# The pools of a Mamba-2 and SiLU kernel in another order in SBUF

## The chip, the cores and the metric

One core of one Trainium2 chip runs the whole program. The metric is device time in microseconds of one execution; a kernel's time is the median of its runs. Profiles are of one execution, taken by the hardware profiler; all engines' times below are from the profile of the kernel before.

## What is computed

First a state-space scan over chunks of the sequence (4 batches, 8 heads, 768 steps, head size 32, state size 16), then two matrix products with a SiLU between them:

```python
for c in range(nc):                       # chunks; log_a = log(clip(a))
    cum = np.cumsum(la, axis=-1)
    L = np.exp(cum[:, :, :, None] - cum[:, :, None, :]) * causal
    M = np.einsum('bhin,bhjn->bhij', Cc, Bc) * L
    y_intra = np.einsum('bhij,bhjd->bhid', M, xc)
    y_inter = np.einsum('bhin,bhnd->bhid', Cc, state) * np.exp(cum)[..., None]
    y[:, :, sl] = y_intra + y_inter
    ...
    state = decay_full[:, :, None, None] * state + np.sum(Bx, axis=2)
x = y.transpose(0, 2, 1, 3).reshape(3072, 256)
h = x @ w_in                              # 256 x 2048
out = (h * (1.0 / (1.0 + np.exp(-h)))) @ w_out    # 2048 x 256
```

x, a, B and C come as float32; the weights come as eight-byte floats, which the kernel turns into float32 on the chip.

## The kernel before

The 3072 tokens are 12 units u of 256 tokens, and 6 pairs G of two units. A unit goes through the scan (f_E, f_B, f_T, f_T2, f_C, f_G, f_M, f_S, f_Y, with small plain-fp32 matmuls at L449, L463, L515 and L524) and ends as a tile ys of outputs. The sixteen weight pieces are loaded into tiles raw (load_w, L210), turned to float32 on ScalarE, VectorE and GpSimd (w_size, w_bits, w_add), and split into parts h, l and d (w_high, w_part), each part of 128x512 numbers in an s2k tile.

The first pair is computed in plain fp32: f_s1 (L573) and f_n2 (L604). All other pairs use fp32r parts. f_XH and f_XL split ys into three xk tiles. s1_mm (L645) multiplies them with the parts of w_in into the PSUM tiles ga and gb: per matmul, 128x128 weights from an s2k slot are held and 512 columns of an xk tile move. ScalarE makes the SiLU and a first part of it (f_a L653, f_d L660, f_h L666), VectorE the two other parts (L531, L534), all in r4k tiles. s2_mm (L626) multiplies these with the parts of w_out into hp and o_ps: again 128x128 weights from an s2k slot, 512 moving columns, now of an r4k tile. There are 480 matmuls at L645 and 480 at L626. f_va, f_vd and f_out (L632, L638, L586) add, transpose and store the result.

The order of everything is written out by hand in the string SCHEDULE: every token is one step, and the steps of all engines and DMA queues are issued in that order. The program is told not to reorder it.

A tile lies in a pool. A pool is a stretch of SBUF; a name (or tag) in it has a number of slots (bufs) that its tiles use in turn. Pools lie one behind the other in the order in which they are opened, and the names of a pool in the order of their first tile, each slot padded to 32 bytes. What goes into which pool, in bytes per partition:

| pool | tiles |
|---|---|
| const | tiny 4, ident 512, diag 2048, hm 32, par 8, one 1040 |
| loads | tbc 2048, bn 1024, pz 1040 |
| loads2 (2 slots each) | ab 4096, xt 2048 |
| rawp (7 slots) | raw 4096; xk uses the same slots |
| sc | ct 1024, ce 2048, cw 1024, BT 1024, bh 1024, sm 1024, bxs 1024, pfx 1040, ys 2048 |
| sc2 (2 slots) | st 1024 |
| sp (49 slots) | s2k, 2048 |
| rp (12 slots) | r4k, 4096 |

In the compiled program of before the first pool starts at byte 16512 of a partition. All slots of s2k and r4k start at 832 modulo 2048; raw (and so xk), ab, xt and ct at 1824; tbc and bn at 1792; ys and st at 832 and up.

Of the kernel before, what the change touches and what calls it, by code (L numbers as in the profile page):

```python
# [8 lines left out]
FP32 = mybir.dt.float32  # L9
# [62 lines left out]
def kernel(  # L72
# [24 lines left out]
    batch, H, S, D = x.shape  # L97
    N = B.shape[-1]
    Q = 64
# [7 lines left out]
    assert (H * N, H * D, D, N) == (128, 256, 32, 16) and S % UT == 0 and d_model == H * D  # L107

    const = ctx.enter_context(tc.tile_pool(name="const", bufs=1))
    loads = ctx.enter_context(tc.tile_pool(name="loads", bufs=1))  # L110
    loads2 = ctx.enter_context(tc.tile_pool(name="loads2", bufs=2))
    rawp = ctx.enter_context(tc.tile_pool(name="rawp", bufs=7))
    sc = ctx.enter_context(tc.tile_pool(name="sc", bufs=1))
    sc2 = ctx.enter_context(tc.tile_pool(name="sc2", bufs=2))
    sp = ctx.enter_context(tc.tile_pool(name="sp", bufs=49))
    rp = ctx.enter_context(tc.tile_pool(name="rp", bufs=12))
    dram = ctx.enter_context(tc.tile_pool(name="dram", bufs=1, space=bass.MemoryType.DRAM))
    ps_s = ctx.enter_context(tc.tile_pool(name="ps_s", bufs=1, space=bass.MemoryType.PSUM))
    ps_h = ctx.enter_context(tc.tile_pool(name="ps_h", bufs=3, space=bass.MemoryType.PSUM))
# [10 lines left out]
    def small(shape, dtype=FP32):  # L130
        return sp.tile(shape, dtype, name="s2k", tag="s2k")
# [7 lines left out]
    bn, tbc, xt, E, M, BT, BH, CT, CE, CW, PFX, ST, SM, DP, BX, YS, PZ = ({} for _ in range(17))  # L139
# [122 lines left out]
    pz01, one01, pfx01 = (large([128, 8 * (Q + 1)]) for _ in range(3))  # L262
    idle = small([128, 512], BF16)
    diag1 = small([128, 1, Q])
    tiny = const.tile([128, 1], FP32, name="tiny")
    ident = const.tile([128, 128], FP32, name="ident")
    diag = const.tile([128, H, Q], FP32, name="diag")
    hm = const.tile([128, H], FP32, name="hm")
    par = const.tile([128, 2], FP32, name="par")
    one = const.tile([128, 4, Q + 1], FP32, name="one")  # L270

    def i_a(l):
        nc.sync.dma_start(out=ach[:, l], in_=bass.AP(tensor=a.tensor, offset=a.offset + l * S,
# [88 lines left out]
            PFX[u] = pfx01.rearrange("p (c t) -> p c t", c=8)[:, 4 * u:4 * u + 4]  # L362

    def f_P(u):
        PFX[u] = sc.tile([128, 4, Q + 1], FP32, name="pfx")
        nc.vector.tensor_tensor_scan(out=PFX[u].rearrange("p c t -> p (c t)"),
                                     data0=PZ[u].rearrange("p c t -> p (c t)"),
                                     data1=one.rearrange("p c t -> p (c t)"), initial=0.0,
                                     op0=ALU.mult, op1=ALU.add)
# [304 lines left out]
    def f_e(G, i):  # L674
# [17 lines left out]
        "ia": i_a, "ip": i_p, "ir": i_r, "ci": c_idle, "ct": c_tiny, "cI": c_ident, "c1": c_diag1, "cd": c_diag,  # L692
        "cp": c_p01, "ch": c_hm, "cP": c_par, "co": c_one, "ca": c_acp, "A": f_A, "AT": f_AT, "AA": f_AA,
        "z": busy, "as": f_AS, "ab": f_Ab, "E": lambda u, *k: f_E(u, k or (0, 1)), "P01": f_P01, "P": f_P,
        "T": f_T, "tp": f_TP, "ce": f_T2, "B": f_B, "C": f_C, "D": lambda u: f_D0(u, True), "g0": f_G0, "G": f_G,
        "b": f_BX, "M": f_M, "S": f_S, "SM": f_SM, "Y": f_Y, "X0": f_X0, "y": f_YS, "xh": f_XH, "x": f_XL,
# [42 lines left out]
```

## Time and profile before

| what | value |
|---|---|
| runs | 345.09, 345.49, 347.36 us; median 345.49 |
| profiled execution, first to last instruction (span) | 345.5 us |
| mean granted TensorE clock | 0.995 |
| VectorE busy | 227.3 us |
| ScalarE busy | 218.5 us |
| moved by DMA | 35.03 MB in 99625 packets |
| first matmul of f_s1 (L573) | at 27.0 us |
| last matmul starts | at 338.5 us |

The span of the profiled execution equals the median of the runs to the tenth, so nothing that has to be counted lies around it. "out<-in xN" names the tile that is written, the tiles that are read, and the number of instructions; PEld is the loading of weights, which runs beside the matmuls. In the groups, the first number behind the bar is busy time in us, the second the mean duration of one in ns; then follows the idle time of the engine ahead of them. In the timeline, the first column is the start in us and the second the time until the last of the row ends; neighbouring matmuls overlap.

### The profile page before, as it was taken

The numbers are of one execution on the slowest core, as the hardware profiler recorded it, in microseconds if no ns is written. First come the engines' busy times: TensorE is split into PE (matmuls) and PEld (weight loads), VectorE is DVE, ScalarE is ACT, GpSimd is POOL, SyncE is SP. The second block draws the span as 40 slices with busy tenths as digits, with TensorE's granted clock in tenths as the row PEclk, the third lists the DMA queues.
The fourth block names the chain that finished last, engine by engine and source line by source line (L and its number), as shares of the span: only waits on it lengthen the run. The fifth ranks groups of instructions, "written<-read, shape, count | busy, mean of one in ns | idle before, by whom it ended". The sixth has DMA issues, their size and how long they took to land.

```text
span 345.5 us, 7609 instructions
## 1 busy us (share of the span) xinstructions
PE 330.6 (96%) x3081; PEld 248.8 (72%) x3082; DVE 227.3 (66%) x310; ACT 218.5 (63%) x339; POOL 75.8 (22%) x96
## 2 busy tenths in 40 slices
PE   5789999999999999999999999999999999999992
PEld 2467875566578777777787787778787788887881
DVE  3957679776356777389778577677675844554553
ACT  3576776757789786775755844647746645557330
POOL 1555336868341245201100010000001000000000
PEclk9999999999999999999999999999999999999998
DMA  5999799799993795985052550561000030012003
GB/s 135 206 198 293 190 300 185 135 166 182 202 157 61 153 177 95 147 154 108 14 91 76 80 107 3 92 138 18 2 0 2 3 60 2 0 29 33 0 0 61
DMA packets 99625, 35.03 MB, mean 101 GB/s; under 512 B 82488, under 2 KB 88632, under 8 KB 99592
## 3 DMA queue, kind: packets, MB, share of 16 engines
q1 hardware_dynamic: 91640, 25.71, 36.7%
q0 software_dynamic: 4784, 8.59, 14.4%
q10 hardware_dynamic: 3168, 0.26, 0.6%
q8 instruction: 24, 0.39, 0.5%
q14 instruction: 9, 0.07, 0.1%
HBM read 22.81 MB, written 3.34 MB: 76 GB/s over the span
## 4 chain that ended last, share of the span: by engine, by line
PE 85%; SPq 5%; DVE 3%; DMA 2%; issue 2%; POOL 1%; ACT 0%; DVEq 0%; POOLq 0%
PE hp L626 27%; PE ga L645 16%; PE gb L645 16%; PE hp L604 8%; PE o_ps L626 5%; PE hp L573 5%; SPq L210 1%; PE ga L463 1%; SPq L176 1%; PE ga L515 1%; PE ga L524 1%; POOL s2k L236 1%; DMA raw<-in_moe_w_in_dram 1%; PE ga L449 1%; PE gb L524 1%
## 5 line engine op out<-in xcount | busy, mean ns | idle before, releaser
L626 PE MATMUL hp<-r4k,s2k 128*128 128x512 f32 x400 | 115.2, 396 | 0.0
L626 PEld LDWEIGHTS hp<-r4k,s2k 128*128 128x128 f32 x400 | 74.3, 188 | 18.3 <-issue 1.3
L531 DVE SCALAR_TENSOR_TENSOR r4k<-r4k 128x1024 fp32r<-128x1024 f32 x40 | 48.8, 1231 | 31.6 <-ACT r4k L666 25.1
L645 PE MATMUL ga<-xk,s2k 128*128 128x512 f32 x240 | 63.9, 401 | 0.5 <-DVE st L494 0.2
L534 DVE SCALAR_TENSOR_TENSOR r4k<-r4k 128x1024 fp32r<-128x1024 f32 x40 | 48.5, 1222 | 22.3 <-ACT r4k L666 20.9
L645 PE MATMUL gb<-xk,s2k 128*128 128x512 f32 x240 | 62.5, 396 | 0.0
L645 PEld LDWEIGHTS ga<-xk,s2k 128*128 128x128 f32 x240 | 44.6, 188 | 13.3 <-ACT bxs L475 2.0
L645 PEld LDWEIGHTS gb<-xk,s2k 128*128 128x128 f32 x240 | 44.7, 188 | 11.3 <-ACT gb L653 0.4
L666 ACT ACTIVATE r4k<-r4k 128x1024 fp32r<-128x1024 f32 x40 | 41.6, 1054 | 0.5
L653 ACT ACTIVATE ga<-ga 128x1024 f32<-128x1024 f32 x20 | 20.2, 1008 | 29.5 <-PE ga L645 29.4
L247 POOL DMA_DIRECT2D s2k<-s2k x32 | 28.7, 1008 | 44.5 <-ACT s2k L245 33.5
L573 PE MATMUL hp<-r4k,s2k 128*128 128x256 f32 x128 | 31.9, 403 | 0.5 <-POOL s2k L236 0.5
L653 ACT ACTIVATE gb<-gb 128x1024 f32<-128x1024 f32 x20 | 20.2, 1008 | 18.4 <-PE gb L645 18.1
L626 PE MATMUL o_ps<-r4k,s2k 128*128 128x512 f32 x80 | 31.0, 394 | 0.0
L573 PEld LDWEIGHTS hp<-r4k,s2k 128*128 128x128 f32 x128 | 25.5, 203 | 7.2 <-issue 2.2
L604 PE MATMUL hp<-r4k,s2k 128*128 128x512 f32 x64 | 29.8, 599 | 0.0
L660 ACT ACTIVATE r4k<-ga 128x1024 f32<-128x1024 f32 x20 | 20.5, 1025 | 13.0 <-PE ga L645 12.3
L396 DVE TENSOR_TENSOR_SCAN ab<-ab,diag 128x512 f32<-128x512 f32 x20 | 25.8, 1309 | 3.2 <-DMA ab<-az 3.2
L236 POOL TENSOR_TENSOR s2k<-s2k 128x512 uint32<-128x512 uint32 (+1 forms) x19 | 24.4, 1318 | 15.6 <-DVE s2k L227 15.6
L404 POOL TENSOR_TENSOR BT<-bn,ab 128x256 f32<-128x256 f32 x10 | 8.3, 833 | 86.5 <-PE ga L645 33.7
L660 ACT ACTIVATE r4k<-gb 128x1024 f32<-128x1024 f32 x20 | 20.5, 1026 | 9.7 <-PE gb L645 8.4
L481 DVE TENSOR_TENSOR ab<-ga,ab 128x512 f32<-128x512 f32 x12 | 8.3, 690 | 18.3 <-PE gb L463 14.2
(111 smaller groups left out, 387.9 us busy)
## 6 DMA issues: line engine op xcount, KB each, us to landing
s2k<-s2k POOLq DMA_DIRECT2D x32, 256.0 KB, 4.7
ab<-az SPq DMA_DIRECT2D x20, 256.0 KB, 5.9
raw<-in_moe_w_in_dram SPq DMA_DIRECT2D x8, 512.0 KB
raw<-in_moe_w_out_dram SPq DMA_DIRECT2D x8, 512.0 KB, 5.3
out_dram<-r4k SPq DMA_DIRECT2D x44, 64.0 KB, 2.0
xt<-in_x_dram SPq DMA_DIRECT2D x20, 128.0 KB, 4.2
pz<-ac SPq DMA_DIRECT2D x10, 130.0 KB
bn<-in_B_dram SPq DMA_DIRECT2D x20, 64.0 KB
```

What stands on the lines that cost most here:

```text
L236: nc.gpsimd.tensor_tensor(out=dst[:, :, fs].bitcast(U32), in0=u[:, :, fs], in1=v[:, :, fs], op=ALU.add)
L247: nc.gpsimd.dma_start(out=f32(t).rearrange("p k f -> p (k f)"), in_=other.rearrange("p k f -> p (k f)"), accum_op=ALU.add)
L396: nc.vector.tensor_tensor_scan(out=o, data0=src, data1=diag.rearrange("p h t -> p (h t)"), initial=0.0, op0=ALU.mult, op1=ALU.add)
L531: nc.vector.scalar_tensor_tensor(out=l, in0=f32(h), scalar=BACK, in1=y, op0=ALU.mult, op1=ALU.add)
L534: nc.vector.scalar_tensor_tensor(out=d, in0=f32(h), scalar=-(BACK + 1.0), in1=y, op0=ALU.mult, op1=ALU.subtract)
L573: nc.tensor.matmul(out=hp[:, i], lhsT=WT[j][:, kc, 128 * i:128 * i + 128], rhs=XM[:, 2 * kc:2 * kc + 2, u], start=(kc == 0), stop=(kc == K ...
L604: nc.tensor.matmul(out=NP["o"][m], lhsT=WT[8 + f // 2][:, f % 2, 128 * m:128 * m + 128], rhs=GT[0, f // 2][:, f % 2], start=(f == 0), stop ...
L626: nc.tensor.matmul(out=ACC[P, 2 * (p == "d") + m], lhsT=WK[8 + f // 2, p][:, f % 2, 128 * m:128 * m + 128], rhs=rhs, start=(f == 0 and p ! ...
L645: nc.tensor.matmul(out=o, lhsT=WK[j, q][:, kc, 128 * i:128 * i + 128], rhs=xs[:, 2 * kc:2 * kc + 2], start=(start and q == "h" and kc == 0 ...
L653: nc.scalar.activation(t, t, AF.Copy, scale=1.0 + Z)
L660: nc.scalar.activation(g, t, AF.Silu, scale=BACK)
L666: nc.scalar.activation(t, GT[G, i], AF.Copy, scale=-LESS * Z)
```

## The change

The pools are opened in another order, and the tiles of const are made ahead of the other pools. A tile of 256 bytes that nobody uses fills const up; diag gets a pool of its own behind rp; pfx moves from sc to loads. Each instruction, each DMA and each wait stays, in the same order. Only the addresses in SBUF are others.

```diff
     const = ctx.enter_context(tc.tile_pool(name="const", bufs=1))
-    loads = ctx.enter_context(tc.tile_pool(name="loads", bufs=1))
-    loads2 = ctx.enter_context(tc.tile_pool(name="loads2", bufs=2))
+    tiny = const.tile([128, 1], FP32, name="tiny")
+    ident = const.tile([128, 128], FP32, name="ident")
+    hm = const.tile([128, H], FP32, name="hm")
+    par = const.tile([128, 2], FP32, name="par")
+    one = const.tile([128, 4, Q + 1], FP32, name="one")
+    const.tile([128, 64], FP32, name="pad")
     rawp = ctx.enter_context(tc.tile_pool(name="rawp", bufs=7))
-    sc = ctx.enter_context(tc.tile_pool(name="sc", bufs=1))
-    sc2 = ctx.enter_context(tc.tile_pool(name="sc2", bufs=2))
     sp = ctx.enter_context(tc.tile_pool(name="sp", bufs=49))
     rp = ctx.enter_context(tc.tile_pool(name="rp", bufs=12))
+    const2 = ctx.enter_context(tc.tile_pool(name="const2", bufs=1))
+    diag = const2.tile([128, H, Q], FP32, name="diag")
+    loads2 = ctx.enter_context(tc.tile_pool(name="loads2", bufs=2))
+    sc2 = ctx.enter_context(tc.tile_pool(name="sc2", bufs=2))
+    sc = ctx.enter_context(tc.tile_pool(name="sc", bufs=1))
+    loads = ctx.enter_context(tc.tile_pool(name="loads", bufs=1))
...
     def f_P(u):
-        PFX[u] = sc.tile([128, 4, Q + 1], FP32, name="pfx")
+        PFX[u] = loads.tile([128, 4, Q + 1], FP32, name="pfx")
```

More of the change, by code (lines that the diff above doesn't have):

```diff
@@ L264 @@
     diag1 = small([128, 1, Q])
[L265 to L270, printed above, removed]
     def i_a(l):
```

## The prediction

> **What bounds the kernel now.** I read the page first, then the windows by stage, then the timeline of TensorE, then the chain at the start. The page says that the kernel is one long TensorE stream at nearly full clock:
>
> ```profile
> span 345.5 us, 7609 instructions
> PE 330.6 (96%) x3081; PEld 248.8 (72%) x3082; DVE 227.3 (66%) x310; ACT 218.5 (63%) x339; POOL 75.8 (22%) x96
> PE 85%; SPq 5%; DVE 3%; DMA 2%; issue 2%; POOL 1%; ACT 0%; DVEq 0%; POOLq 0%
> L626 PE MATMUL hp<-r4k,s2k 128*128 128x512 f32 x400 | 115.2, 396 | 0.0
> L645 PE MATMUL ga<-xk,s2k 128*128 128x512 f32 x240 | 63.9, 401 | 0.5 <-DVE st L494 0.2
> L645 PE MATMUL gb<-xk,s2k 128*128 128x512 f32 x240 | 62.5, 396 | 0.0
> L626 PE MATMUL o_ps<-r4k,s2k 128*128 128x512 f32 x80 | 31.0, 394 | 0.0
> ```
>
> PE is on 85% of the chain, and the idle column of its large groups is near zero. The mean of 396 ns is one matmul from entry to end; matmuls overlap, so what counts is the distance from one start to the next. The timeline gives it. Two stretches, the first of L645 and then L626, the second of L626 alone:
>
> ```profile
> 198.21 2.03 PE L645 MATMUL gb<-xk,s2k 128*128 128x512 f32 x8
> 200.08 2.03 PE L645 MATMUL ga<-xk,s2k 128*128 128x512 f32 x8
> 201.94 1.09 PE L626 MATMUL hp<-r4k,s2k 128*128 128x512 f32 x4
> 202.87 0.39 PE L626 MATMUL o_ps<-r4k,s2k 128*128 128x512 f32 x1
> ```
> ```profile
> 217.35 0.39 PE L626 MATMUL hp<-r4k,s2k 128*128 128x512 f32 x1
> 217.58 0.39 PE L626 MATMUL o_ps<-r4k,s2k 128*128 128x512 f32 x1
> 217.81 1.30 PE L626 MATMUL hp<-r4k,s2k 128*128 128x512 f32 x5
> 218.94 0.39 PE L626 MATMUL o_ps<-r4k,s2k 128*128 128x512 f32 x1
> 219.17 1.07 PE L626 MATMUL hp<-r4k,s2k 128*128 128x512 f32 x4
> ```
>
> The reader is to divide. Sixteen L645 take 201.94 - 198.21 = 3.73 us, 233 ns each. Eight L626 take 219.17 - 217.35 = 1.82 us, 227.5 ns each. The four L626 straight after L645 take 0.93 us, 232 ns each. Both are the same instruction: 128 rows, 512 contiguous fp32r columns, 128x128 weights from s2k, full clock. Taken over the whole trace, by the starts of neighbours (steps under 260 ns, so no waits): 468 steps after an L645 have mean 233.2 ns and alternate between 235 and 232; 445 steps after an L626 have mean 229.6; and L626 from the sixth place of a run on has mean 227.3. The first five places after an L645 run have medians 230, 235, 228, 232 and 230. Neither the half of the tile, nor the quarter of the weights, nor the bank, nor what DVE, ACT or POOL do at that moment explains more than a nanosecond of it. What does differ is where the moving operand lies. In the compiled program of before, s2k and r4k start at 832 modulo 2048 (0 modulo 64); raw, from whose slots xk comes, starts at 1824 modulo 2048 (32 modulo 64).
>
> The start, up to the first L573 at 27 us, hangs on SyncE's issues and on DMAs. This is the sum by line of the chain from 0 to 27 us:
>
> ```profile
> by line: SPq L210 19.0%; SPq L176 18.5%; DMA raw<-in_moe_w_in_dram 16.3%; DMA s2k<-in_x_dram 11.0%; SPq L281 8.7%; SPq L191 7.9%; SPq L273 5.8%; issue 4.2%; DVE st L496 3.2%; PE hp L449 2.5%; DVEq L496 0.2%
> ```
>
> **The change part by part.** Nothing is removed or added: each instruction, DMA, wait and queue position stays; no step moves past another on any queue. Only addresses differ. Pools start at byte 16512. The new const holds 32 + 512 + 32 + 32 + 1056 + 256 = 1920 bytes, so rawp starts at 18432 = 9 x 2048, sp at 47104 = 23 x 2048, rp at 147456 = 72 x 2048; diag, ab, xt, st follow on multiples too, then sc, then loads. One thing falls short of the words: in sc the order of first use is ct (1024 bytes), then ce (2048), so ce lands 1024 past a multiple. It is read by short L463 matmuls and I cost that at nothing.
>
> 1. L645, moving operand from 1824 to 0 modulo 2048. 480 matmuls. After the change their operands stand to each other as L626's do now (moving start and weight slot equal modulo 2048), and both start on a multiple of 64. I take L626's settled step: 480 x (233.2 - 227.3) = 2.8 us less. Bounds: no gain (if the address is not the cause), or an estimate from the plain fp32 matmuls: L573 and L604 take 0.84 ns per column (216 for 256, 430 for 512), L626 0.444; half of 0.84 is 0.42, or 215 ns for 512, which I take as the lower end: 480 x 18.2 = 8.7 us. I take 227.3, the nearest row, same form and same engine state.
>
> 2. L626, from 832 to 0 modulo 2048. Its 229.6 is 227.3 plus the slow first places after L645. If L645 no longer leaves the stream in another rhythm, these go: 480 x 2.3 = 1.1 us less. Bounds: 0 (the first places after a pause are slow as well, 231, 235, 229, 232, so part of it may be a refill that any change of line brings), and 480 x (229.6 - 215) = 7.0 us by the same lower end. I take 1.1, since the pattern follows L645 on 55 occasions and pauses on 14.
>
> 3. Plain fp32 matmuls, L573 and L604: 216 and 430 ns, 0 modulo 64 already. Nothing. Small ones (L449, L463, L515, L524) sit 6 to 7 ns apart and together take some 24 us after 42 us; their operands come from 32 to 0 modulo 64. Their steps are set by issue, four at a time; the bounds are nothing and, at the 2.5% of point 1, 0.6 us. I take nothing.
>
> 4. DVE, ACT and POOL work on the same tiles. The like copies L245 (s2k to s2k, 624 ns) and L557 (ys to xk, 629 ns) differ by 5 ns, and L557 is the one at 32 modulo 64: nothing per instruction, at most 10 x 5 ns. DVE is busy 66% and ACT 63% beside a PE that does not wait for them: in the windows from 280 to 320 us PE is never idle. If PE runs 1.2% faster, what is late next is the chain ACT L653, L660, L666, DVE L531, L534; it has over 30% of slack in these windows and the order of the program keeps several items ahead, so I charge nothing. Without that cover, every late item costs what the 340 ns steps do now, some 100 ns each, 14 of them in L626.
>
> 5. DMA into raw, s2k, r4k, xt, bn. After 42 us hidden behind PE. Before 27 us it is on the path: the first raw load 4.41 us, and SyncE issues of up to 2.38 us that stand behind a busy queue. Bounds: none, or a tenth of the roughly 15 us that wait for DMA, 1.5 us either way, taken from the spread of equal raw loads (4.8 to 5.8 us to landing). I take nothing. [...]
>
> Sum against the profiled span of 345.5, which equals the median of the runs shown (345.49): 345.5 - 2.8 - 1.1 = 341.6, less a little that 3 and 5 may add. I say 341.5.
>
> **Rivals.**
>
> *The address is not the cause, 345.3.* L645 differs from L626 in more than the address: it goes on in one two-bank tile, and its weights step by 1024 bytes. For it: I have no row with the same line at two addresses. Against it: same-bank and other-bank neighbours of L626 differ by 0.4 ns, of L645 by 0.7. [...]
>
> *Alignment beyond 64 pays too, 330.* L626 now starts 64 past a multiple of 128 and 256. Should its own 227.3 fall to 215 as well: 8.7 + 7.0 = 15.7 us, 330. For it: 12 ns per matmul that twice the rate of plain fp32 would not have. Against it: nothing says that fp32r must reach exactly that rate, and no row starts on 128 or more.
>
> *Equal residues collide, slower.* All 68 large slots now begin at one residue, raw among them, so the moving stream, the weight load and DVE and ACT on other slots more often stand at the same place. If each 128x512 lost one more step of 5.9 ns: 960 x 5.9 = 5.7 us, 351. It decides from a mean step above 231.4 ns (the present mean of both lines); 1% slower is 235.0. Against it: s2k and r4k share 832 now, and that is the fast line; steps of L626 do not grow when DVE or ACT is busy (fitted 0.2 and 0.6 ns).
>
> **How the numbers follow.** Forecast (340.3 to 342.4 for itself) 0.50; no effect 0.22; deeper alignment 0.14; collision 0.14. The predicted time is the first. A measurement here tells about 1% from no change, so 342.0 and 349.0 are the lines. The forecast gives faster in three of four (0.38), the rest within 1%; deeper gives 0.14 faster. Together faster 0.52, within 1% 0.34, slower 0.14. The range goes from 337.0, a little beyond half of a deeper gain (345.5 - 7.9 = 337.6), to 347.0, which holds no effect with a DMA loss of 1.5 us; it leaves out most of deeper and of collision, 0.2 in all.
>
> **What would show it.** Right: L645's start-to-start step at 227 to 228 and no slow places behind it, L626 at 227 to 228, starts of the first L573 within 1 us of 27, no new wait of PE. Wrong: L645 still at 233 (rival one), L626 under 225 (two), any of them above 235 (three); a new row of PE waiting for ACT L653 or DVE L534 would say that the cover of point 4 was thinner than I took it, and a first L573 moved by over 1 us that point 5 was.

## The result, and the profile after

The changed kernel takes 341.46 us (median of 4, 340.02 to 343.88), the kernel before 345.29 (median of 4, 344.78 to 347.36): ratio 0.9871, 95% interval 0.9832 to 0.9910. Run once more with more rounds (341.50 against 346.36) the ratio is 0.9867, interval 0.9844 to 0.9889. So it is faster by 1.3%, some 4 us. The ratios below leave out one execution of 372.9 us, of the third kernel of the experiments, in which TensorE was granted 0.83 of its clock.

One reading of the time before has to be mended. A run's time is 2.0 us more than its span: 340.9 and 338.9 us for the profiled execution after, 346.5 and 344.5 for a second profile of the kernel before. The execution before that was profiled with a span of 345.5 therefore took about 347.5 us, two above the median. The two first profiles differ by 6.6 us of span; the medians differ by only about four.

These are the lines of the page after that answer to those of before. Line numbers have moved by two: L626 is L628, L645 is L647, L573 is L575.

```profile
span 338.9 us, 7609 instructions
PE 322.5 (95%) x3081; PEld 245.0 (72%) x3082; DVE 227.0 (67%) x310; ACT 218.2 (64%) x339; POOL 75.8 (22%) x96
PE 86%; SPq 5%; DVE 3%; issue 2%; POOL 1%; DMA 1%; ACT 0%; DVEq 0%; POOLq 0%
L628 PE MATMUL hp<-r4k,s2k 128*128 128x512 f32 x400 | 114.5, 395 | 0.0
L647 PE MATMUL ga<-xk,s2k 128*128 128x512 f32 x240 | 62.7, 396 | 0.5 <-DVE st L496 0.2
L647 PE MATMUL gb<-xk,s2k 128*128 128x512 f32 x240 | 61.2, 390 | 0.0
L628 PE MATMUL o_ps<-r4k,s2k 128*128 128x512 f32 x80 | 30.9, 393 | 0.0
```

TensorE lost 8 us of busy time, 3.3 of them in the four fp32r groups shown, the rest in the first pair and the start. DVE, ACT and POOL kept theirs to 0.3 us. The two stretches of the timeline that answer to those of before:

```profile
193.81 1.98 PE L647 MATMUL gb<-xk,s2k 128*128 128x512 f32 x8
195.63 1.98 PE L647 MATMUL ga<-xk,s2k 128*128 128x512 f32 x8
197.44 1.07 PE L628 MATMUL hp<-r4k,s2k 128*128 128x512 f32 x4
198.35 0.39 PE L628 MATMUL o_ps<-r4k,s2k 128*128 128x512 f32 x1
198.57 1.30 PE L628 MATMUL hp<-r4k,s2k 128*128 128x512 f32 x5
199.71 0.61 PE L647 MATMUL ga<-xk,s2k 128*128 128x512 f32 x2
```

Sixteen L647 now take 197.44 - 193.81 = 3.63 us, 227 ns each (233 before), and the four L628 behind them 0.91 us, 227 each (232 before). Over the trace the mean step is 227.7 ns for either line, before 233.3 and 229.6; the first places of L628 behind L647 all have the median 227.

Where the time went, by three stretches of the traces (us; two profiles of the kernel before, four of the layout after, since two kernels below begin with the whole changed kernel):

```
                                          before          after
start to first matmul of f_s1             27.0  26.1      24.9  27.0  26.1  25.6
from there to first s1_mm (first pair)    53.5  53.4      52.5  52.7  52.9  52.4
from there to the end of TensorE          258.5 258.4     255.1 255.3
```

The last row is the gain of the steps, 3.3 us, and stands still between executions. The start is different in every execution and shows no gain: the 2.1 us that the first two profiles differ by there are spread. The first pair is shorter by 0.8 on average, but this is not shown to be the layout's. It goes with the granted clock. These are TensorE's rows from 25 to 30 us and the durations at f_s1 (shortest/median/longest, ns), first of the second profile of the kernel before, then of the first one after. In the first kind of row, the number behind the bracket is the granted clock:

```profile
25.00:30.00 5.00, 5.00 (x48) 0.50 1.02 350
L573 PE MATMUL hp<-r4k,s2k x128: 379/379/795, 26.1 to 90.4; 128*128 128x256 f32 x128
25.00:30.00 5.00, 4.89 (x22) 1.00 0.98 340
L575 PE MATMUL hp<-r4k,s2k x128: 379/379/483, 24.9 to 88.2; 128*128 128x256 f32 x128
```

Where f_s1 begins while the clock stands at half, its matmuls step by 427 ns; at the full clock they step by 216 (in the first profile of before the clock is on record only from 31.5 us on, which is where its steps of 427 end). Ten matmuls of f_s1 were slow in either profile of before, and 0, 6, 7 and 3 in the four of after. In the kernels of the experiments below it is anything from 0 to 10. Without this loss the first pair takes 51.2 to 51.3 us in both profiles of before, and 51.2, 51.3 and 51.5 in three of the four after. The fourth lost nothing to the clock, but has waits instead, one of 0.4 us for a DMA. So 3.3 us of the gain are shown to be the layout's; the rest of the difference of the medians, 0.5 us in the first set of runs and 1.6 in the second, lies in a part where executions of one kernel differ by more.

### The profile page after: what moved, and what is told of

The parts are those of the page before. It is cut to its first block, busy times and chain, and to the rows that moved or that the text cites. A ratio compares the mean times of both kernels' runs of the same rounds, so it can differ in the third digit from the quotient of the medians.

```text
span 338.9 us, 7609 instructions
## 1 busy us (share of the span) xinstructions
PE 322.5 (95%) x3081; PEld 245.0 (72%) x3082; DVE 227.0 (67%) x310; ACT 218.2 (64%) x339; POOL 75.8 (22%) x96
## 4 chain that ended last, share of the span: by engine, by line
PE 86%; SPq 5%; DVE 3%; issue 2%; POOL 1%; DMA 1%; ACT 0%; DVEq 0%; POOLq 0%
PE hp L628 27%; PE ga L647 16%; PE gb L647 16%; PE hp L606 8%; PE o_ps L628 5%; PE hp L575 5%; SPq L184 2%; PE ga L465 2%; PE ga L517 1%; SPq L218 1%; PE ga L526 1%; POOL s2k L244 1%; PE ga L451 1%; PE gb L526 1%; DVE ab L483 1%
## 5 line engine op out<-in xcount | busy, mean ns | idle before, releaser
L628 PE MATMUL hp<-r4k,s2k 128*128 128x512 f32 x400 | 114.5, 395 | 0.0
L628 PEld LDWEIGHTS hp<-r4k,s2k 128*128 128x128 f32 x400 | 74.2, 188 | 17.4 <-issue 1.3
L533 DVE SCALAR_TENSOR_TENSOR r4k<-r4k 128x1024 fp32r<-128x1024 f32 x40 | 48.8, 1230 | 30.6 <-ACT r4k L668 24.6
L647 PE MATMUL ga<-xk,s2k 128*128 128x512 f32 x240 | 62.7, 396 | 0.5 <-DVE st L496 0.2
L647 PE MATMUL gb<-xk,s2k 128*128 128x512 f32 x240 | 61.2, 390 | 0.0
L647 PEld LDWEIGHTS ga<-xk,s2k 128*128 128x128 f32 x240 | 44.5, 188 | 12.4 <-ACT bxs L477 2.0
L647 PEld LDWEIGHTS gb<-xk,s2k 128*128 128x128 f32 x240 | 44.6, 188 | 10.3 <-ACT gb L655 0.9
L628 PE MATMUL o_ps<-r4k,s2k 128*128 128x512 f32 x80 | 30.9, 393 | 0.0
L575 PE MATMUL hp<-r4k,s2k 128*128 128x256 f32 x128 | 30.0, 384 | 0.6 <-POOL s2k L244 0.5
L575 PEld LDWEIGHTS hp<-r4k,s2k 128*128 128x128 f32 x128 | 23.8, 190 | 7.0 <-issue 2.3
L398 DVE TENSOR_TENSOR_SCAN ab<-ab,diag 128x512 f32<-128x512 f32 x20 | 25.8, 1309 | 3.3 <-DMA ab<-az 3.3
```

The source lines that it names most:

```text
L398: nc.vector.tensor_tensor_scan(out=o, data0=src, data1=diag.rearrange("p h t -> p (h t)"), initial=0.0, op0=ALU.mult, op1=ALU.add)
L533: nc.vector.scalar_tensor_tensor(out=l, in0=f32(h), scalar=BACK, in1=y, op0=ALU.mult, op1=ALU.add)
L575: nc.tensor.matmul(out=hp[:, i], lhsT=WT[j][:, kc, 128 * i:128 * i + 128], rhs=XM[:, 2 * kc:2 * kc + 2, u], start=(kc == 0), stop=(kc == K ...
L628: nc.tensor.matmul(out=ACC[P, 2 * (p == "d") + m], lhsT=WK[8 + f // 2, p][:, f % 2, 128 * m:128 * m + 128], rhs=rhs, start=(f == 0 and p ! ...
L647: nc.tensor.matmul(out=o, lhsT=WK[j, q][:, kc, 128 * i:128 * i + 128], rhs=xs[:, 2 * kc:2 * kc + 2], start=(start and q == "h" and kc == 0 ...
```

## The experiments

The prediction's first point held two conditions side by side, and the change sets both. Theory A takes one: a moving operand must start on 64 bytes (a multiple of 64; "on 64" in what follows). Theory B takes the other: moving operand and weights must lie equally modulo 2048. Theory C: part of the gain is DMA into the first tiles.

**The raw slots alone moved off.**

```diff
-    rawp = ctx.enter_context(tc.tile_pool(name="rawp", bufs=7))
     sp = ctx.enter_context(tc.tile_pool(name="sp", bufs=49))
...
     loads = ctx.enter_context(tc.tile_pool(name="loads", bufs=1))
+    gap = ctx.enter_context(tc.tile_pool(name="gap", bufs=1))
+    gap.tile([128, 8], FP32, name="gap")
+    rawp = ctx.enter_context(tc.tile_pool(name="rawp", bufs=7))
```

> The changed kernel, but the raw (and xk) slots alone lie behind all other pools and start at 1120 modulo 2048, 32 modulo 64. Theory A (the moving operand of a matmul must start on 64 bytes): the L645 step goes back to 233 ns, the first L626 after L645 to 230 to 235, L626 settles at 227; 480 x 5.9 + 480 x 2.3 = 3.9 us lost, about 345.3. Theory B (moving operand and weights must lie equally modulo 2048): the same, since 1120 differs from 0. Theory C (part of the gain is DMA into the first tiles, 2 us at the start): if raw is what DMA needs on a multiple, the first L573 moves from 24.9 back to 27 us as well, about 347; by A and B alone it stays within 1 us of 25.

Measured: 346.28 us, ratio to the kernel before 1.0013 (0.9992 to 1.0034). Steps 233.7 for s1_mm and 230.5 for s2_mm. Moving this one pool undoes the whole gain, and the slow first places of s2_mm come back. The first f_s1 matmul is at 25.8 us: nothing for C.

**The same without the 32 bytes**, so raw on a multiple of 64:

> As the run before, without the 32 bytes: raw and xk start at 1088 modulo 2048, which is 0 modulo 64, all else at multiples of 2048. A: L645 keeps 227 to 228 ns, no slow first places, the time stays at 341.5. B: 1088 differs from 0, so L645 goes to 233, about 345.3. No effect of the address at all: as the changed kernel in both.

Measured: 344.88 us, ratio 0.9966 (0.9945 to 0.9987); steps 230.8 and 230.1. Neither theory: A wants 227 and the whole gain, B wants 233 and none. A multiple of 64 is not enough.

**The pools in the old order, all large tiles on 64.**

```diff
+    gap = ctx.enter_context(tc.tile_pool(name="gap", bufs=1))
+    gap.tile([128, 8], FP32, name="gap")
     loads = ctx.enter_context(tc.tile_pool(name="loads", bufs=1))
...
+    gap2 = ctx.enter_context(tc.tile_pool(name="gap2", bufs=1))
+    gap2.tile([128, 8], FP32, name="gap2")
     sp = ctx.enter_context(tc.tile_pool(name="sp", bufs=49))
```

> The kernel before with 32 bytes ahead of loads and 32 ahead of sp: raw and xk at 1856, s2k and r4k at 896 modulo 2048, all 0 modulo 64, the pools in the old order. A: L645 at 227 to 228, L626 at 227 to 228, 341.5. B: raw differs from s2k by 960, L645 stays at 233, 345.3. C: the PE steps fall but the start does not gain (first L573 at 27 us), about 343.4; by A with an unstable start it may lie at 25 or 27.

Measured: 345.69 us, ratio 0.9991 (0.9967 to 1.0015); steps 233.0 and 230.1. A falls. The first f_s1 matmul is at 25.0 us, with the pools in the old order, so an early start does not need the new one. The timeline of this kernel (s1_mm is L649 here, s2_mm L630):

```profile
197.91 2.03 PE L649 MATMUL gb<-xk,s2k 128*128 128x512 f32 x8
199.78 2.03 PE L649 MATMUL ga<-xk,s2k 128*128 128x512 f32 x8
201.65 1.08 PE L630 MATMUL hp<-r4k,s2k 128*128 128x512 f32 x4
```

Sixteen in 3.74 us, 234 ns each, with xk, r4k and s2k all on 64.

**The weights moved off, the moving operands left on multiples.**

```diff
     rawp = ctx.enter_context(tc.tile_pool(name="rawp", bufs=7))
-    sp = ctx.enter_context(tc.tile_pool(name="sp", bufs=49))
...
     loads = ctx.enter_context(tc.tile_pool(name="loads", bufs=1))
+    gap = ctx.enter_context(tc.tile_pool(name="gap", bufs=1))
+    gap.tile([128, 8], FP32, name="gap")
+    sp = ctx.enter_context(tc.tile_pool(name="sp", bufs=49))
```

> The changed kernel, but the s2k slots lie behind all other pools and start at 1120 modulo 2048, 32 modulo 64: the weights of all matmuls move off, the moving operands stay on multiples. A: weights do not matter, both steps stay at 227, 341.5. B: all 960 matmuls have unequal addresses, 960 x 5.9 = 5.7 us more, 347. C: the first x, a, B and C tiles lie in s2k, so if DMA needs them aligned the first L573 goes from 24.9 to 27 us, 343.5 on top of A.

Measured: 349.27 us, ratio 1.0088 (1.0063 to 1.0114): slower than the kernel before. Steps 234.2 and 234.3, s2_mm too:

```profile
195.56 2.03 PE L649 MATMUL gb<-xk,s2k 128*128 128x512 f32 x8
197.43 2.04 PE L649 MATMUL ga<-xk,s2k 128*128 128x512 f32 x8
199.31 1.10 PE L630 MATMUL hp<-r4k,s2k 128*128 128x512 f32 x4
200.25 0.40 PE L630 MATMUL o_ps<-r4k,s2k 128*128 128x512 f32 x1
200.48 1.33 PE L630 MATMUL hp<-r4k,s2k 128*128 128x512 f32 x5
```

Against the kernel before, 480 x 0.9 and 480 x 4.7 ns more make 2.7 us, 0.8%, about what was measured. (The profiled execution itself took 346.36 us, the fastest of ten; only one of its f_s1 matmuls met the half clock.) The first f_s1 matmul is at 26.1 us, within the spread, so nothing for C. The weights' place counts as much as the moving operand's. What is left is the distance between the two starts; call this theory D.

**992 unused bytes in the kernel before**, which bring s2k and r4k to the place of raw, none of them on 64:

```diff
+    gap = ctx.enter_context(tc.tile_pool(name="gap", bufs=1))
+    gap.tile([128, 248], FP32, name="gap")
     sp = ctx.enter_context(tc.tile_pool(name="sp", bufs=49))
```

> The kernel before with one unused tile of 992 bytes ahead of sp and nothing else: raw, xk, s2k and r4k all start at 1824 modulo 2048, which is 32 modulo 64. Theory A (absolute alignment) has fallen with the run in which all were 0 modulo 64 and L645 stayed at 233; alignment on 128 or more, its remaining form, expects 233 or more for both lines here, 346 or above. Theory D (the distance from the weights' start to the moving start, modulo 512, sets the step; equal is best) expects 227 to 228 for both lines, no slow first places, and a ratio to the kernel before of 0.989 (3.6 us less).

Measured: 342.45 us, ratio 0.9894 (0.9870 to 0.9918); steps 227.9 and 228.0.

```profile
195.47 1.98 PE L647 MATMUL gb<-xk,s2k 128*128 128x512 f32 x8
197.29 1.98 PE L647 MATMUL ga<-xk,s2k 128*128 128x512 f32 x8
199.10 1.07 PE L628 MATMUL hp<-r4k,s2k 128*128 128x512 f32 x4
```

Sixteen in 3.63 us, with every operand at 32 modulo 64. With the distance at 0 the step is the good one, though nothing is on 64.

**Series of matmuls at chosen distances**, behind the changed kernel:

```diff
     f_s2(len(S2))
+    G, i = NPAIR - 1, NF // 2 - 1
+    flat = HT[G, i].rearrange("p k c -> p (k c)")
+    wt = WK[15, "l"].rearrange("p k f -> p (k f)")
+    for m0, w0 in [(0, 0), (8, 8), ... (0, 256), (0, 0)]:
+        t = ps_h.tile([128, 512], FP32, name="hp")
+        for n in range(20):
+            nc.tensor.matmul(out=t, lhsT=wt[:, w0:w0 + 128], rhs=flat[:, m0:m0 + 512], start=True, stop=True,
+                             skip_group_check=True)
```

> The changed kernel followed by 23 series of 20 equal fp32r matmuls of 128 rows and 512 columns, moving operand and weights starting so many columns past a multiple of 2048 bytes; they add some 106 us and their result is used for nothing. D: series with equal shifts, (8, 8), (16, 16), (64, 64), step as (0, 0), 227; unequal ones between 229 and 236, the same for 128 and 256 columns (multiples of 512 bytes) as for 0. Absolute alignment: (8, 8) and (16, 16) are slow, (64, 0) and (0, 64) as fast as (0, 0).

Two stretches of its timeline, the series (8, 8) and the series (8, 0), each with one matmul of the series ahead of it:

```profile
338.27 4.96 PE L716 MATMUL hp<-r4k,s2k 128*128 128x512 f32 x21
356.57 5.07 PE L716 MATMUL hp<-r4k,s2k 128*128 128x512 f32 x21
```

Both shift the moving operand by 32 bytes; only where the weights shift along is the series short. Worked out from the starts, in ns: the mean step from the seventh to the nineteenth of a series, by bytes from the weights' start to the moving start:

```
distance 0, both shifted by 0 / 32 / 64 / 256      226.6  227.0  227.0  226.6
moving ahead by 16 / 32 / 64 / 96 / 128 / 192      231.4  233.1  228.6  233.8  233.6  233.2
moving ahead by 256 / 512 / 1024                   226.7  226.6  226.7
moving ahead by 384                                233.6
weights ahead by 16 / 32 / 64 / 128 / 384          226.7  233.5  233.5  232.4  232.6
weights ahead by 256 / 512 / 1024                  226.7  226.7  226.7
```

D holds in these series, and its period is 256 bytes, not 512: every multiple of 256 tried (0, 256, 512 and 1024) gives 226.6 to 227.0, the other distances 228.6 to 233.8, but for weights 16 bytes ahead (226.7).

**224 unused bytes in the kernel before**, to try the period in place; the edit is that of the 992 bytes, with 56 columns for 248:

> The kernel before with one unused tile of 224 bytes ahead of sp: raw and xk stay at 1824 modulo 2048, s2k and r4k go to 1056, so the distance from weights to moving operand at L645 is 768, three times 256, and nothing large is on a multiple of 64. Theory D with the period of 256 bytes that the series showed: L645 and L626 at 227 to 228, ratio to the kernel before 0.989. A condition of 512 or 2048 bytes on the distance: L645 at 233, ratio 1.000.

Measured: 343.42 us, ratio 0.9912 (0.9882 to 0.9943); steps 227.8 and 228.0. The period is 256 bytes in place too. Distances in the table are modulo 256, worked out from the addresses, and the last column is the series at the distance of s1_mm, from the first set or the second, which follows. Kernels and series agree within 1.5 ns, but for distance 64, where the kernel's 230.8 lies 2 ns above the series:

```
kernel                    s1_mm at  step     s2_mm at  step     series there
before                    224       233.3    0         229.6    233.5 (weights ahead by 32)
raw moved, 32 off         96        233.7    0         230.5    233.8
raw moved, on 64          64        230.8    0         230.1    228.6
all on 64                 192       233.0    0         230.1    233.2
weights moved, 32 off     160       234.2    160       234.3    234.1
after                     0         227.7    0         227.7    226.6
992 bytes                 0         227.9    0         228.0    226.6
224 bytes                 0         227.8    0         228.0    226.6
```

Where s1_mm alone is off, s2_mm at distance 0 still pays 2 to 3 ns: these are its first places behind s1_mm.

**What the clash is.** The second set of series takes more distances, fewer weight columns, and alternating weights.

> The changed kernel followed by series of 20 fp32r matmuls, result used for nothing: sixteen with the moving operand 0, 16, 32 to 240 bytes past the weights, then with 64 and with 32 weight columns at distance 0 and 128, then with weights alternating between 0 and 128 bytes under a moving operand at 0 and at 128. D as a clash of two reads: 227 at distance 0, 229 to 234 at all others, perhaps less just around 0; narrower weights are read in less time, so the step at 128 falls towards that at 0, and if the 227 itself holds a clash, that falls too, towards 215. If the distance to the next matmul's weights counts (they are loaded while this one runs), the alternating series have long steps where the next weights are off; if the own ones count, where the own are off.

Measured: in steps of 16 bytes from 0 to 240 the step is 226.7, 231.3, 233.2, 233.5, 228.6, 230.9, 233.6, 230.6, 233.0, 233.3, 234.1, 233.3, 233.5, 234.8, 233.5, 226.7. So of these sixteen places 0 and 240, 16 bytes below the next multiple of 256, are the good ones, with 226.7. The part on width failed: 64 weight columns step by 230.5 at distance 0 and 229.0 at 128, 32 columns by 231.8 and 231.2. Narrower weights cost more at distance 0, though their loads are shorter (134 and 108 ns for 188), and no series got below 226.6. Alternating weights gave 232.5 and 232.0, mixed over both places, so they don't tell whether the matmul's own or the next one's weights count.

The seams of the first set say more on this. The trace shows the weights of the next matmul being loaded beside the one that runs: the load for the first matmul of (8, 8) starts 4 ns after the last matmul of (0, 0). Five well-placed series are followed by one whose weights lie at a bad distance from the moving operand still running. Their last matmul steps by 235, 235, 235, 232 and, at distance 64, 226 ns; where the next weights lie well, it steps by 226 or 227, also when both addresses change. Four cases of five speak for the next weights, the ones being loaded; more was not tried.

**Both kernels once more**, for the spread of the start and more rounds:

> The kernel before, unchanged, for a second profile: the steps by line again 233 and 229.6. If the 2.1 us by which the changed kernel's start was shorter belong to the addresses, the first L573 is again at 27 us; if they are spread between executions, it may be anywhere from 25 to 27.

> The changed kernel, unchanged, with more rounds beside the run with 992 bytes: steps of 227 to 228, ratio to the kernel before 0.988 to 0.990. If alignment of the other tiles is worth something beyond the distance, it is faster than the run with 992 bytes; by D alone the two are equal within 0.2%.

Measured: before, steps 233.2 and 229.6, first f_s1 matmul at 26.1 us; after, steps 227.9 and 227.9, first f_s1 matmul at 27.0 us, ratio 0.9867 (0.9844 to 0.9889). The start is spread in both. The ratio with 992 bytes is 0.9894 (0.9870 to 0.9918): the intervals overlap, so a further gain from the other tiles' alignment is not shown.

## Why the prediction was right, and where its reasons were not

*Point 1, s1_mm* was right in size: 480 x (233.3 - 227.7) = 2.7 us for the 2.8 forecast. Its working had two conditions in it, equal places modulo 2048 and a start on 64. The first is what counts, modulo 256 and not 2048 (227.8 with the distance of s1_mm at 768); the second does nothing by these runs: 233.0 with all on 64 and s1_mm at 192, 227.9 with none on 64 and s1_mm at 0. Where the prediction said what differs, it named "where the moving operand lies", each start by itself; it is the distance to the weights. It came out because the change sets both, so the agreement of point 1 did not tell the two apart.

*Point 2, s2_mm* was right too: 480 x (229.6 - 227.7) = 0.9 for 1.1. The slow first places of s2_mm, medians of 228 to 235 behind s1_mm before, come where s1_mm is off, and are 227 where it is not. Behind its pauses they stay, as the bound allowed: the first three steps behind the waiting one have medians of 236, 233 and 233 ns in the first profile after, 231, 236 and 229 in the second.

*Points 3 and 4* hold. Plain fp32 at full clock keeps its median steps in every layout, 216 ns at f_s1 and 429 at f_n2. The small matmuls take 23.9 us after 42 us in the first profile of either kernel. All of L515 (L517 after) start in fours, 5 to 8 ns apart and then a step of 38 or more, about nine in ten of L449 and L463 in eights; that issue sets these steps was the author's reading. DVE L531 takes 1231 ns before and 1230 after, and the new waits of TensorE in the first profile are three single ones: 0.8 us at L517 for ACT L505, 0.5 at L465 for ACT L547, 0.4 at L417 for a DMA into bn.

*Point 5, DMA at nothing,* stands as far as these runs go. By the prediction's own sign, a first L573 moved by over 1 us, it would have failed: 24.9 for 27.0 us. The repeats undo this sign, since the same two kernels start f_s1 at 26.1 and 27.0 as well. The first pair's 0.8 us go with the clock, as shown above. Some packets did get shorter: those of 128 bytes from SyncE, which are x loads and output stores, took a mean of 13.5 ns in both profiles before and 12.5 to 12.6 in the four after, those of 2 KB 115 to 117 and 105 to 109. No run isolates the reason, or turns it into time.

*The sum* hit the time, 341.5 for 341.46, more closely than it had a right to. It started from 345.5 as if span and time were one, and the steps' 3.9 us came out as 3.6 by the means and as 3.3 in the whole stretch from the first s1_mm to the end of TensorE; the start and the first pair, at nothing in the sum, made up the rest in these executions.

*No effect of the address* fell with the first experiment: with nothing but the raw slots moved, s1_mm stepped by 233.7 ns for 227.7. The series need less than that: with the moving operand 16 bytes ahead of the weights the step is 231 ns, 16 bytes behind them 227. With the same tiles, form and count, they go from 227 to 234 ns by nothing but the distance between the two starts.

*Alignment beyond 64* fell: at multiples of 2048 the settled step is the 227 that 832 had, and with all at 32 modulo 64 the means are 228 as well. *Equal residues collide* was the wrong way round. Equal residues are the good case, and unequal ones cost the step of 6 ns that this rival charged; the run with the weights moved off shows what it would have been, 0.9% slower.

Open: what in the chip has the period of 256 bytes. That weight reads and moving reads get in each other's way is argued from the distance alone, with the four seams in its favour, and the series with narrower weights speak against the simple form in which the clash lasts as long as the weight read.

## What to carry to other kernels

Where fp32r matmuls follow each other at full rate (measured here for 128x128 weights and 512 columns), place the moving tiles and the weight tiles so that the distance of their starts is a multiple of 256 bytes; here an unused tile of 224 bytes bought 0.9%, and weights at a wrong distance cost 0.9%. Read the rate from start to start, since the mean duration of an overlapped matmul is another number (395 ns for hp after the change, at a mean step of 227.7), and when two lines with one instruction form differ by nanoseconds, list the addresses of both operands, not of one.

## What was not expected of the hardware

A 128x512 fp32r matmul steps by 226.6 ns at best, by the means of the series; the lower end that the prediction estimated, half of the 430 ns of plain fp32, was 215, and no distance, alignment or width of weights tried here reached it. In the series the effect of a bad distance outlasts its cause: behind a badly placed series, or behind a single bad seam, a well-placed series steps by 224 to 237 ns for up to nine matmuls before it settles at 227. The plain fp32 matmuls here do not show the effect: in the one layout that puts their weights off (weights moved, distance 160) they step by 216 ns for 256 columns and 429 for 512, as in the others.
